# A lane-pipelined attention and MoE kernel: hand-overs between lanes are deferred, whole-array work is gathered into fewer pauses, and the order table is replaced

## The chip, the cores and the metric

The kernel runs on one core of a Trainium2 chip. TensorE (PE) multiplies, VectorE (DVE) and ScalarE (ACT) empty PSUM, GpSimd (POOL) scales the results and issues most of the transfers, and SyncE (SP) issues the others. The time is the device time of one execution in microseconds (us); lower is better. Three executions of the kernel before took 563.68, 565.47 and 568.73 us, so their median is 565.47 us.

## The reference

The input `x` is 4 batches of 12480 tokens with 128 features. There are 32 inducing points, and a feed-forward layer of width 2048 with a PReLU between its two products:

```python
def mab(q, kv):
    s = scale * (q @ kv.transpose(0, 2, 1))
    s = s - s.max(-1, keepdims=True)
    a = np.exp(s)
    a /= a.sum(-1, keepdims=True) + 1e-09
    return a @ kv
h = mab(I, x)                 # 32 rows of 128 for each batch
out = mab(x, h)               # 12480 rows of 128 for each batch
# feed-forward on all 49920 tokens
h = out @ w_in                # 128 -> 2048
g = np.maximum(h, 0.0) + alpha * np.minimum(h, 0.0)
result = g @ w_out            # 2048 -> 128
```

## The kernel before, in words

**The algebra.** For every batch the kernel first makes `h` (32 x 128), then multiplies it with `w_in` (`h_weights`, L458) to `hW`, 16 chunks of 32 x 128. Tokens are worked on in groups of 512, `g`, 24 whole ones and one of 192 in a batch. For a group the exponentials of the 32 scores of each token stand in a tile `rep`, copied four times over the 128 partitions, so that each 32-row strip of the PE array has its own copy. One matmul of 32 rows gives one chunk of the hidden layer, 128 x 512, in a PSUM bank. This is a *fill* (L595). ACT (L613) or DVE (L616) takes the ReLU of it into a `gt` buffer in SBUF. PReLU is split as ReLU times `W1 = (1 - alpha) w_out` plus a linear part, `hA`, that needs no hidden layer (`linear`, L634). The division by the sum of the exponentials comes last: DVE transposes the finished group (L663), POOL multiplies by the reciprocals `rdT` (L666), and four DMAs write it (L680).

**The lanes.** The 32-row strips of the array are four lanes, 0 to 3, that work beside one another. The second product of a group needs 128 rows of every `gt`; each lane holds a quarter. So a group is accumulated in its own PSUM bank in four passes: 16 *pieces* (L620) in lane 0, then 16 in lane 1, and so on. Four groups are under way, each in another lane. Fills are put into whichever lane has room. Since two lanes must not write one bank at once, a group that ends its pass in lane `f` is *handed over*: the kernel places a PE drain that raises the semaphore `fence` (L1061), and the first piece in lane `f + 1` waits for that value (L1054). A drain is declared as fusable. In the built program 261 of 276 hand-overs ride on the last matmul of the pass and 15 stay as an instruction of their own, in front of a PE instruction that waits for something.

**The pauses.** The work for the next batch and for later groups (transposes of `x`, scores, pooling, denominators, `h`) needs the whole array, not lanes. It is put into `tasks` by group number (L844, with the schedule in L860 to L905). When a group starts in lane 0 and its number has such work, all lanes stop, the work runs, and the lanes go on (`pause`, L951, L1012). The 192-token group at the end of a batch (`wholes`, L827 to L832) is also computed on the whole array in such pauses, half of its eight double chunks in one pause and half in the next.

**What sets the order.** A planner inside the kernel (`tokens`, L817) writes out the order of every PE instruction. It keeps rough clocks of PE, ACT and DVE, lists what could be issued next, and takes the earliest. Three knobs for each group (`KNOBS`, L34) say how eager it is to fill, how little must be left of the pass in lane 3 before a fourth group enters, and what a fill costs in a lane that has a pass; the letters of `PLAN` (L35) choose the knobs group by group. Up to `KEPT` = 66 `gt` buffers can be filled ahead. After a hand-over the flag `closed` (L1063) asks for a piece that waits for nothing as the next instruction (a *calm* one); if there is none it takes another. *Warm* matmuls (L1036), 63 of them, write into unused banks while lanes 2 and 3 are still empty.

**Queues.** Each engine runs its instructions in order. SP issues, among others, the copies of exponentials to DRAM and back (`rep`, L516), the reciprocals (`rdT`, L559) and the DMA transposes of `x` (L191); POOL issues the loads of `x` (L177) and nearly all writes of results. The last four groups (L677 to L679) are written by SP, or by SP and ACT in turn.

**The end.** After the last lane pass the last two whole groups and the last 192-token group are computed on the whole array (`tail`, L833).

Of the kernel before, what the change touches and what calls it, by code (L numbers as in the profile page):

```python
# [17 lines left out]
P = 128  # L18
# [6 lines left out]
TAIL = 2  # L25
AHEAD = 8
LAND = 8000
KEPT = 66
RDS = 4
SLOT = 217  # L30
XTS = 8
DONE = 420
SWITCH = 110
KNOBS = [(h, r, c) for h in (300, 450, 600, 800, 1100) for r in (16, 10, 6, 3) for c in (0, 60)]  # L34
PLAN = (  # L35
    "yqbyysrquizoaHqiuiiiobNbizFqbhjiFawqweqiyqiiDbqy"
    "iqqimNqihauihaFicikaebaoaaxiaFbgahiiiaDakiki"
)


# [1 line left out]
def kernel(  # L42
# [9 lines left out]
    nc = tc.nc  # L52
    f32 = mybir.dt.float32
# [80 lines left out]
    def mm(o, lhsT, rhs, start=True, stop=True, **kw):  # L134
        return pin(nc.tensor.matmul(o, lhsT, rhs, start=start, stop=stop, **kw))  # L135
# [302 lines left out]
        st.xn.pop(u)  # L438

    def h_make(st):  # L440
        st.et = work.tile([P, 1], f32, name="et", tag="et")
        pin(nc.vector.tensor_scalar_mul(
            out=st.et[:], in0=st.hacct[:, C : C + 1], scalar1=1.0 / scale
        ))
        ps = bank()
        mm(ps[:, :P], st.hacct[:, :C], fold[:])
        st.hT4 = work.tile([C, P], bf16, name="hT4", tag="hT4")
        pin(nc.vector.tensor_copy(out=st.hT4[:], in_=ps[:, :P]))
        drained(ps, "D", 250, 300)
        st.hT = st.hT4[:, 0:M]  # L450
        ps = bank()
        mm(ps[:, 0:1], fold[:], st.et[:])
        st.rs = work.tile([P, 1], f32, name="rs", tag="rs")
        st.sc = st.rs
        pin(nc.vector.reciprocal(out=st.rs[:], in_=ps[:, 0:1]))
        drained(ps, "D", 150, 100)

    def h_weights(st):  # L458
        st.hW = hw_pool.tile([P, KC, P], bf16, name="hW", tag="hW")
# [108 lines left out]
    begun = set()  # L568
    seen = {}
    held = []  # L570

    def units(g):
        return KC // shape_of(g)[2]
# [78 lines left out]
    def finish(b, g):  # L652
        st = states[b]
        pp, nb, _ = shape_of(g)
        t = pp * nb
        acc = acc_of(b, g)
        s, q = divmod(g, NQ)
        rq = st.rden[s][:, :, :, q : q + 1]
        rbc = bass.AP(
            tensor=rq.tensor, offset=rq.offset, ap=[rq.ap[0], rq.ap[1], rq.ap[2], [0, 32]]  # L660
        )
        ot = ot_pool.tile([P, GRP], f32, name="ot", tag="ot")
        pin(nc.vector.transpose(out=ot[:, :t], in_=acc[:, :t]))  # L663
        drained(accs[b, g], "D", 74 + t * 1.04)
        ob = ob_pool.tile([P, GRP], f32, name="ob", tag="ob")
        pin(nc.gpsimd.tensor_tensor(  # L666
            out=ob[:, :t].rearrange("p (k m c) -> p k m c", k=nb, c=32),
            in0=ot[:, :t].rearrange("p (k m c) -> p k m c", k=nb, c=32),
            in1=rbc, op=MULT,
        ))  # L670
        t0 = b * N + s * SUP
        if s < NS:
            dst = out[t0 : t0 + SUP, :].rearrange(
                "(i b q) (a k) -> q a i b k", b=t // 32, q=NQ, k=32)[q]
        else:
            dst = out[t0 : t0 + REM, :].rearrange("(i b) (a k) -> a i b k", b=t // 32, k=32)
        ending = b == B - 1 and g >= NG - 4  # L677
        for a in range(4):
            eng = (nc.sync, nc.scalar)[a % 2] if ending and g >= NG - 3 else nc.sync if ending else nc.gpsimd  # L679
            pin(eng.dma_start(  # L680
                out=dst[a],
                in_=ob[32 * a : 32 * a + 32, :t].rearrange("p (b k) -> p b k", k=32),
            ))
        st.rep.pop(g)

    order = [0, 1, NS] + list(range(2, NS))
# [130 lines left out]
    def tokens(st):  # L817
# [10 lines left out]
        for b in range(B - 1):  # L828
            c = first[b + 1, 0] - 1
            first[b, NG - 1] = c  # L830
            for u in range(units(NG - 1)):
                wholes[c + u * 2 // units(NG - 1)].append((b, NG - 1, u))  # L832
        tail = [y for y in direct[2:] if y[0] == B - 1]  # L833
        tail.sort()
        need = [((first[y], 1, u), (*y, u)) for y in laned for u in range(KC)]
# [22 lines left out]
        for b in range(B):  # L858
            base = T0 + (first[b, 0] if b else -2)
            for s in range(1, NS + 1):  # L860
                t = base + 4 * s - AHEAD if b or s > 2 else 4 * s - 2
                nt = t + 4 if s < NS else t + 2
                at(t, lambda b=b, s=s: b_scores(states[b], s))
                at(t + 1, lambda b=b, s=s: b_rep(states[b], s))
                at(nt, lambda b=b, s=s: b_den(states[b], s))
                at(nt + 1, lambda b=b, s=s: b_turn(states[b], s))
            if b + 1 < B:
                n = b + 1
                E = base + 4 * NS
                if b:  # L870
                    lag = (-8, -4, -4, 0, 4, 8, 10) if b > 1 else (-4, 0, 0, 4, 6, 8, 10)
                    score = [base + k for k in lag]
                    load = [t - 7 for t in score]
                    cross = [t - 5 for t in score]
                else:
                    score = [T0 + k for k in (2, 4, 4, 6, 9, 11, 13)]
                    load = [0, 0, 5, SESSIONS, T0 + 2, T0 + 4, T0 + 6]
                    cross = [None, None, 6, T0 + 1, T0 + 4, T0 + 6, T0 + 8]
                    at(7, lambda: p_xpose(states[1], 0, 0))
                    at(SESSIONS, lambda: p_xpose(states[1], 0, 1))  # L880
                    at(T0 + 2, lambda: p_xpose(states[1], 1, 0))
                    at(T0 + 3, lambda: p_xpose(states[1], 1, 1))
# [9 lines left out]
                if n == 1:  # L892
                    at(H + 1, lambda n=n: h_make(states[n]))
                    H += 2
                else:
                    at(score[-1] + 1, lambda n=n: h_sum(states[n]))
                    at(H, lambda n=n: h_den(states[n]))
                    at(H + 1, lambda n=n: h_transpose(states[n]))
                    H += 2
                assert H <= E - 6  # L900
                at(H, lambda n=n: h_weights(states[n]))
                at(H, lambda n=n: b_scores(states[n], 0))
# [7 lines left out]
        def run_tasks(t):  # L910
            for fn in tasks.pop(t, []):
                fn()

        prior = []
        for t in range(SESSIONS):
            now = [(0, t // 4, 4 * (t % 4) + f) for f in range(4)]
# [25 lines left out]
        moving = []  # L942
        free_at = [clk.pe] * 4
        gate = {}
        closed = False
        hungry_at, room, cost = 600, KC, 0
        plans = list(PLAN)
        assert len(plans) == len(laned)
        fresh = {f: bank() for f in (2, 3)}
# [1 line left out]
        def pause(t):  # L951
            return t in pauses or (t - T0 < len(wholes) and wholes[t - T0])
# [4 lines left out]
            b, g, _ = need[0]  # L957
            return b in states and g in states[b].rep and hasattr(states[b], "hW")

        while queue or moving or any(tile):  # L960
            best = []
            taken = {q for _, q, _ in moving}
            for f in range(4):
                if tile[f]:
                    y, todo = tile[f]
# [5 lines left out]
                else:  # L971
                    for y, q, t in moving:
                        if q == f:
                            best.append((max(free_at[f], t), 1, f, "enter"))
                    lanes = sum(map(bool, tile)) + len(moving)
                    if f == 0 and queue and lanes < LANES and (
                        lanes < LANES - 1 or room == KC or tile[3] and len(tile[3][1]) <= room
                    ):
# [14 lines left out]
            for f in sorted(fresh):  # L993
                if soon and f not in taken:
                    best.append((free_at[f], 9, f, "warm"))
            assert best, (need[:2], len(seen), tile, moving, queue[:2])
            if closed:
                calm = [x for x in best if x[3] == "piece" and x[2] and x[2] not in gate]
                calm += [x for x in best if x[3] == "warm"]
                best = calm or [x for x in best if x[3] == "piece"] or best  # L1000
            t, _, f, what, *_ = min(best, key=lambda x: (max(x[0], clk.pe) + sum(x[4:]), x[1]))
            if what == "start" and plans:
                m = first[queue[0]]
                if len(laned) - len(plans) == m:
                    hungry_at, room, cost = KNOBS[string.ascii_letters.index(plans.pop(0))]
                    continue
            closed = False
            clk.pe = max(clk.pe, t)
            rows = slice(32 * f, 32 * f + 32)
            if what == "start":  # L1010
                m = first[queue[0]]
# [14 lines left out]
            if what == "enter":  # L1026
# [6 lines left out]
                    clk.free[i] = clk.pe + SLOT  # L1033
                    idle.append(i)
                continue
            if what == "warm":  # L1036
                mm(
                    fresh[f][:], W1[rows, 0, :],
                    W1[rows, 0:NB, :].rearrange("p k c -> p (k c)"), skip_group_check=True,
                )  # L1040
                free_at[f] = clk.pe + SLOT
                continue
            if what == "fill":
                fill(need.pop(0), f)
            else:
# [4 lines left out]
                else:  # L1050
# [7 lines left out]
                    if not todo:  # L1058
                        tile[f] = None
                        if f < 3:  # L1060
                            pin(nc.tensor.drain(fusable=True)).then_inc(fence, 1)  # L1061
                            fenced += 1
                            closed = True  # L1063
                            fences[y, f + 1] = fenced
                            moving.append((y, f + 1, clk.pe + DONE))
                        flush()
            free_at[f] = clk.pe + SLOT
        clk.pe = max(clk.pe, max(free_at) + SWITCH)
        for t in sorted(tasks):
            run_tasks(t)  # L1070
        for y in tail:
# [43 lines left out]
```

## Time and profile before

| | |
|---|---|
| executions | 563.68, 565.47, 568.73 us |
| profiled execution, its own time | 570.99 us |
| its span, first to last instruction | 569.2 us |
| PE busy | 546.6 us (96%), 8860 matmuls |
| ACT busy | 505.3 us (89%) |
| DVE busy | 500.4 us (88%) |
| POOL busy | 408.7 us (72%) |
| mean granted clock of TensorE | 0.988 |
| separate PE drains at L1061 | 15 |

An engine's busy time is the time in which at least one of its instructions was in work. Matmuls overlap, four lanes at a time, so that a busy PE can still have empty lanes: at full pace a 32-row matmul of 512 columns starts every 53 to 54 ns (four in 216 ns), while the profile gives each a duration of 376 ns. ACT takes 617 ns for a full chunk (901 instructions) and DVE 679 ns (635). The granted clock is 1.00 except in short stretches at 0.50.

### The profile page before, as it was taken

Reading aid. Unit: us, or ns where it says so; the run is one execution under the profiler, and the core shown is the slowest. Engines: PE = TensorE matmul, PEld = TensorE weight load, DVE = VectorE, ACT = ScalarE, POOL = GpSimd, SP = SyncE. Lnnn points to the kernel's source line nnn. Section 1 sums busy time; section 2 is a strip of 40 time slices with the busy share of each in tenths; the row PEclk is TensorE's granted clock in tenths of the full one; section 3 lists DMA queues with packets and bytes.
Section 4 is the critical chain, followed back from the end, with each engine's and each line's share of the span. In section 5 each row is a group of like instructions: output and inputs, shape, how many; then the busy total and the mean of one; then the engine's idle time right before and its main releaser. Section 6 shows DMA issues by size and latency. Waiting matters only on the chain.

```text
span 569.2 us, 21360 instructions
## 1 busy us (share of the span) xinstructions
PE 546.6 (96%) x8860; PEld 295.4 (52%) x8864; DVE 500.4 (88%) x861; ACT 505.3 (89%) x1005; POOL 408.7 (72%) x600
## 2 busy tenths in 40 slices
PE   4999997999999999999999999999999999999995
PEld 4645553455455454454555565455555454474642
DVE  3689995899998999999999999999989999999971
ACT  2479995998999999999999999999999999999970
POOL 6646574676688997785987976865778777668681
PEclk9999997999999999999999999999999999999988
DMA  9976999555599997866796894333344244243233
GB/s 198 225 145 125 144 168 157 101 119 82 108 190 159 165 170 142 149 129 107 138 176 123 161 181 115 77 89 68 86 95 113 59 105 102 54 97 66 53 62 62
DMA packets 111201, 69.25 MB, mean 122 GB/s; under 512 B 79824, under 2 KB 101696, under 8 KB 111104
## 3 DMA queue, kind: packets, MB, share of 16 engines
q0 software_dynamic: 23280, 38.53, 36.4%
q1 hardware_dynamic: 85152, 28.52, 26.8%
q8 instruction: 69, 1.13, 0.9%
q10 hardware_dynamic: 2672, 0.84, 0.6%
q14 instruction: 28, 0.23, 0.1%
HBM read 41.00 MB, written 28.95 MB: 123 GB/s over the span
## 4 chain that ended last, share of the span: by engine, by line
POOL 35%; PE 32%; issue 20%; PEld 5%; DVE 4%; DMA 2%; POOLq 0%; SPq 0%; PEldq 0%; ACT 0%; DVEq 0%
PE bank L135 30%; POOL out_dram L680 23%; POOL ob L666 11%; PEld L135 5%; DVE gt L616 2%; PE bank L223 2%; POOL xn L177 1%; DMA ind_f<-in_inducing_dram 1%; DMA rep<-e2d 1%; DVE ot L663 1%; DVE hW L310 1%; DMA out_dram<-ob 0%; DVE xT L229 0%; POOLq L666 0%; PEldq L1061 0%
## 5 line engine op out<-in xcount | busy, mean ns | idle before, releaser
L135 PE MATMUL bank<-gt,W 32*128 32x512 bf16 (+2 forms) x6013 | 490.7, 376 | 4.3 <-issue 3.6
L613 ACT ACTIVATE gt<-bank 128x512 bf16<-128x512 f32 (+1 forms) x920 | 470.2, 615 | 23.9 <-PE bank L135 19.6
L616 DVE TENSOR_SCALAR gt<-bank 128x512 bf16<-128x512 f32 (+1 forms) x648 | 406.6, 677 | 26.8 <-PE bank L135 22.7
L135 PE MATMUL bank<-rep,hW 32*128 32x512 bf16 (+1 forms) x1600 | 415.5, 370 | 2.4 <-DVE hW L310 0.3
L135 PEld LDWEIGHTS <-W 32*128 32x128 bf16 (+1 forms) x6079 | 228.9, 92 | 188.5 <-issue 114.6
L680 POOL DMA_DIRECT2D out_dram<-ob x384 | 246.2, 672 | 43.0 <-POOL ob L666 28.9
L666 POOL TENSOR_TENSOR ob<-ot,rdT 128x512 f32<-128x512 f32 (+1 forms) x100 | 109.4, 1094 | 100.4 <-DVE ot L663 88.8
L135 PEld LDWEIGHTS <-hW 32*128 32x128 bf16 x1600 | 134.0, 92 | 36.7 <-issue 18.6
L663 DVE STREAM_TRANSPOSE ot<-bank 128x512 f32<-128x512 f32 (+1 forms) x100 | 69.7, 698 | 19.0 <-PE bank L135 18.0
L177 POOL DMA_DIRECT2D xn<-in_x_dram x70 | 40.2, 648 | 4.6 <-DMA xn<-in_x_dram 2.4
L135 PE MATMUL bank<-rep,hA 32*128 32x512 bf16 x94 | 35.3, 379 | 0.3 <-DVE hW L310 0.3
L229 DVE COPY xT<-bank 128x1024 bf16<-128x1024 bf16 (+1 forms) x16 | 10.7, 672 | 4.7 <-PE bank L223 4.6
L250 ACT ACTIVATE e1t<-bank 128x256 bf16<-128x256 f32 (+1 forms) x13 | 4.8, 371 | 9.9 <-PE bank L135 8.7
L135 PEld LDWEIGHTS <-hA 32*128 32x128 bf16 x94 | 8.5, 91 | 7.1 <-issue 5.3
L223 PE MATMUL bank<-ident,xn 128*128 128x128 bf16 x128 | 11.3, 242 | 0.9 <-DVE xn L781 0.9
L135 PE MATMUL bank<-xT,hT 128*32 128x512 bf16 (+1 forms) x98 | 10.4, 389 | 0.4 <-ACT gt L613 0.4
L135 PE MATMUL bank<-W 32*128 32x512 bf16 x63 | 10.3, 376 | 0.0
L498 ACT ACTIVATE e<-bank,rs 128x512 bf16<-128x512 f32 x12 | 8.5, 708 | 1.8 <-PE bank L135 1.7
L223 PEld LDWEIGHTS <-xn 128*128 128x128 bf16 x128 | 8.7, 109 | 2.1 <-DVE xn L781 1.0
L498 ACT ACTIVATE e<-bank 128x512 bf16<-128x512 f32 x12 | 7.5, 626 | 1.9 <-PE bank L135 1.8
L135 PE MATMUL bank<-IT,xT 128*128 128x32 bf16 x192 | 8.0, 179 | 0.6 <-issue 0.4
L135 PEld LDWEIGHTS <-e 128*128 128x128 bf16 x96 | 4.3, 96 | 7.4 <-issue 7.4
(100 smaller groups left out, 145.4 us busy)
## 6 DMA issues: line engine op xcount, KB each, us to landing
out_dram<-ob POOLq DMA_DIRECT2D x372, 64.0 KB, 2.7
rep<-e2d SPq DMA_DIRECT2D x92, 128.0 KB, 3.6
xn<-in_x_dram POOLq DMA_DIRECT2D x48, 128.0 KB, 5.8
xn<-in_x_dram POOLq DMA_DIRECT2D x22, 256.0 KB, 7.4
e2d<-e SPq DMA_DIRECT2D x24, 128.0 KB, 2.9
rdT<-rt SPq DMA_DIRECT2D x96, 8.0 KB, 2.2
w_out_f<-in_moe_w_out_dram POOLq DMA_DIRECT2D x4, 256.0 KB, 11.1
xs<-in_x_dram SPq DMA_DIRECT2D x1, 512.0 KB, 5.0
```

Source lines behind the costliest of these rows:

```text
L135: return pin(nc.tensor.matmul(o, lhsT, rhs, start=start, stop=stop, **kw))
L177: pin(nc.gpsimd.dma_start(out=xn[:, i * w : (i + 1) * w, :], in_=src[:, i * w : (i + 1) * w, :]))
L223: pin(nc.tensor.transpose(tp[:, k * P : (k + 1) * P], xn[:, q, j * C : (j + 1) * C], ident[:]))
L229: pin(nc.vector.tensor_copy(out=dst, in_=tp[:, :w]))
L250: pin(nc.scalar.activation(out=e1t[:pp, :nb, :].rearrange("p k m -> p (k m)"), in_=ps[:pp, : nb * M], func=EXP, scale=scale,))
L310: pin(nc.vector.tensor_scalar(out=out, in0=in_, scalar1=st.rs[:, 0:1], scalar2=1.0 / scale, op0=MULT, op1=MULT,))
L498: pin(nc.scalar.activation(out=e2[:].rearrange("p (t j i) -> p t j i", j=n, i=32), in_=turned(ps[:pp, :w], n), func=EXP, scale=scale_of(st ...
L613: pin(nc.scalar.activation(out=gt[:, :w], in_=ps[:, :w], func=RELU))
L616: pin(nc.vector.tensor_relu(gt[:, :w], ps[:, :w]))
L663: pin(nc.vector.transpose(out=ot[:, :t], in_=acc[:, :t]))
L666: pin(nc.gpsimd.tensor_tensor(out=ob[:, :t].rearrange("p (k m c) -> p k m c", k=nb, c=32), in0=ot[:, :t].rearrange("p (k m c) -> p k m c", ...
L680: pin(eng.dma_start(out=dst[a], in_=ob[32 * a : 32 * a + 32, :t].rearrange("p (b k) -> p b k", k=32),))
```

## The change

- **Hand-overs.** A finished pass goes into a list `owed`. `hand_over()` places the drain just before the next calm matmul (a piece that waits for nothing, a warm or a spare one), before a pause, or when nothing else can be issued. A fourth knob, `at_once`, lets a group hand over without a calm matmul, and the planner's clock then counts `DRAIN` = 270 ns.
- **Pauses.** Tasks are moved by one or two group numbers so that they share a pause; the eight double chunks of a 192-token group go into one pause instead of two. Loads and transposes of `x` move by up to two groups.
- **Buffers and table.** `KEPT` 66 to 62, `XTS` (buffers for transposed `x`) 8 to 9; new `KNOBS` and a new `PLAN`. The planner is told that groups 2 and 3 of batch 0 land at 9000 ns.
- **The end.** While the last pieces run, *spare* matmuls with no use fill the lanes below. Of the four DMAs that write the last 512-token group (`NG - 2` of the last batch), two are kept back and issued by POOL after those of the last 192-token group (`NG - 1`).
- **h_make** (the first pass over batch 1's sums) multiplies by the scale after the reciprocal instead of before the matmul.

```diff
-KEPT = 66
+KEPT = 62
-XTS = 8
+XTS = 9
+DRAIN = 270
-KNOBS = [(h, r, c) for h in (300, 450, 600, 800, 1100) for r in (16, 10, 6, 3) for c in (0, 60)]
+KNOBS = [
+    (h, r, c, d) for h in (300, 450, 600, 800) for r in (16, 6, 3) for c in (0, 60) for d in (0, 1)
+]
...
     def h_make(st):
-        st.et = work.tile([P, 1], f32, name="et", tag="et")
-        pin(nc.vector.tensor_scalar_mul(
-            out=st.et[:], in0=st.hacct[:, C : C + 1], scalar1=1.0 / scale
-        ))
...
-        mm(ps[:, 0:1], fold[:], st.et[:])
+        mm(ps[:, 0:1], fold[:], st.hacct[:, C : C + 1])
...
+        pin(nc.vector.tensor_scalar_mul(out=st.rs[:], in0=st.rs[:], scalar1=scale))
...
+            src = ob[32 * a : 32 * a + 32, :t].rearrange("p (b k) -> p b k", k=32)
+            if b == B - 1 and g == NG - 2 and a > 1:
+                late.append((dst[a], src))
+            else:
+                pin(eng.dma_start(out=dst[a], in_=src))
+        if b == B - 1 and g == NG - 1:
+            for dst, src in late:
+                pin(nc.gpsimd.dma_start(out=dst, in_=src))
...
-                wholes[c + u * 2 // units(NG - 1)].append((b, NG - 1, u))
+                wholes[c + 1].append((b, NG - 1, u))
...
-                t = base + 4 * s - AHEAD if b or s > 2 else 4 * s - 2
-                nt = t + 4 if s < NS else t + 2
+                t = base + 4 * s - AHEAD - (b == 0 and s > 4) if b or s > 2 else 4 * s - 2
+                nt = t + (5 if b == 0 and s == 2 else 3 if b == 0 and s == 4 else 4 if s < NS or b + 1 < B else 2)
...
-                    lag = (-8, -4, -4, 0, 4, 8, 10) if b > 1 else (-4, 0, 0, 4, 6, 8, 10)
+                    lag = (-8, -4, -4, 0, 4, 8, 8) if b > 1 else (-4, 0, 0, 4, 4, 8, 8)
-                    load = [t - 7 for t in score]
-                    cross = [t - 5 for t in score]
+                    load = [t + k - 7 for t, k in zip(score, (0, 0, 2, 0, 1, 0, 2))]
+                    cross = [t + k - 5 for t, k in zip(score, (0, 0, 1, 0, 1, 0, 2))]
...
-                    cross = [None, None, 6, T0 + 1, T0 + 4, T0 + 6, T0 + 8]
+                    cross = [None, None, 6, T0 + 1, T0 + 4, T0 + 7, T0 + 8]
...
-                    at(H + 1, lambda n=n: h_transpose(states[n]))
-                    H += 2
+                    at(H + 2, lambda n=n: h_transpose(states[n]))
+                    H += 4
...
+        landed.update({(0, g): 9000 for g in (2, 3)})
...
+        def hand_over():
+            nonlocal fenced
+            if owed:
+                pin(nc.tensor.drain(fusable=True)).then_inc(fence, 1)
+                fenced += 1
+            for y, f in owed:
+                fences[y, f + 1] = fenced
+                moving.append((y, f + 1, clk.pe + DONE))
+            owed.clear()
...
+            if not queue and not need:
+                low = min([f for f in range(4) if tile[f]] + sorted(taken), default=4)
+                for f in range(low):
+                    best.append((free_at[f], 9, f, "spare"))
+            calm = [x for x in best if x[3] == "piece" and x[2] and x[2] not in gate]
+            calm += [x for x in best if x[3] in ("warm", "spare")]
+            if owed and not best:
+                hand_over()
+                continue
+            if owed and not calm and at_once:
+                hand_over()
+                clk.pe += DRAIN
+                continue
...
-            if closed:
-                calm = [x for x in best if x[3] == "piece" and x[2] and x[2] not in gate]
-                calm += [x for x in best if x[3] == "warm"]
-                best = calm or [x for x in best if x[3] == "piece"] or best
+            if owed and calm:
+                best = calm
...
+            if best is calm or what == "start" and pause(T0 + first[queue[0]]):
+                hand_over()
...
-                            pin(nc.tensor.drain(fusable=True)).then_inc(fence, 1)
-                            fenced += 1
-                            closed = True
-                            fences[y, f + 1] = fenced
-                            moving.append((y, f + 1, clk.pe + DONE))
+                            owed.append((y, f))
```

More of the change, by code (lines that the diff above doesn't have):

```diff
@@ L27 @@
 LAND = 8000
-KEPT = 66
+KEPT = 62
 RDS = 4
 SLOT = 217
-XTS = 8
+XTS = 9
 DONE = 420
 SWITCH = 110
-KNOBS = [(h, r, c) for h in (300, 450, 600, 800, 1100) for r in (16, 10, 6, 3) for c in (0, 60)]
+DRAIN = 270
+KNOBS = [
+    (h, r, c, d) for h in (300, 450, 600, 800) for r in (16, 6, 3) for c in (0, 60) for d in (0, 1)
+]
 PLAN = (
-    "yqbyysrquizoaHqiuiiiobNbizFqbhjiFawqweqiyqiiDbqy"
-    "iqqimNqihauihaFicikaebaoaaxiaFbgahiiiaDakiki"
+    "aaKKfGcyLqmADMamiiznjafamQcyaqcafqanqaxacmOaav"
+    "AmnCamKeacfymraaJmRnAynqyauaNmmgadjmafycQazyAm"
 )
@@ L455, in h_make @@
         pin(nc.vector.reciprocal(out=st.rs[:], in_=ps[:, 0:1]))
-        drained(ps, "D", 150, 100)
+        pin(nc.vector.tensor_scalar_mul(out=st.rs[:], in0=st.rs[:], scalar1=scale))
+        drained(ps, "D", 250, 100)
     def h_weights(st):
@@ L570 @@
     held = []
+    late = []
     def units(g):
@@ L679, in finish @@
             eng = (nc.sync, nc.scalar)[a % 2] if ending and g >= NG - 3 else nc.sync if ending else nc.gpsimd
[L680 to L683, printed above, removed]
+            src = ob[32 * a : 32 * a + 32, :t].rearrange("p (b k) -> p b k", k=32)
[6 more added lines that the diff above has]
+                pin(nc.gpsimd.dma_start(out=dst, in_=src))
         st.rep.pop(g)
@@ L944, in tokens @@
         gate = {}
-        closed = False
-        hungry_at, room, cost = 600, KC, 0
+        owed = []
+        hungry_at, room, cost, at_once = 600, KC, 0, 0
         plans = list(PLAN)
@@ L958, in fillable @@
             return b in states and g in states[b].rep and hasattr(states[b], "hW")
-        while queue or moving or any(tile):
+        def hand_over():
[7 more added lines that the diff above has]
+            owed.clear()
+        while queue or moving or owed or any(tile):
             best = []
-            taken = {q for _, q, _ in moving}
+            taken = {q for _, q, _ in moving} | {f + 1 for _, f in owed}
             for f in range(4):
@@ L974, in tokens @@
                             best.append((max(free_at[f], t), 1, f, "enter"))
-                    lanes = sum(map(bool, tile)) + len(moving)
+                    lanes = sum(map(bool, tile)) + len(moving) + len(owed)
                     if f == 0 and queue and lanes < LANES and (
@@ L1004, in tokens @@
                 if len(laned) - len(plans) == m:
-                    hungry_at, room, cost = KNOBS[string.ascii_letters.index(plans.pop(0))]
+                    hungry_at, room, cost, at_once = KNOBS[string.ascii_letters.index(plans.pop(0))]
                     continue
-            closed = False
             clk.pe = max(clk.pe, t)
+            if best is calm or what == "start" and pause(T0 + first[queue[0]]):
+                hand_over()
             rows = slice(32 * f, 32 * f + 32)
@@ L1035, in tokens @@
                 continue
-            if what == "warm":
+            if what == "spare" and f not in fresh:
+                fresh[f] = bank()
+            if what in ("warm", "spare"):
                 mm(
@@ L1068, in tokens @@
         clk.pe = max(clk.pe, max(free_at) + SWITCH)
+        for f in sorted(fresh):
+            i = number[id(fresh.pop(f))]
+            clk.free[i] = clk.pe
+            idle.append(i)
         for t in sorted(tasks):
```

## The prediction

> **What bounds the kernel now.** I read the stretches first, then the waits inside the lanes, then single pauses and drains on PE. The busy time by stretches (columns: stretch, its length, busy us and instructions of PE, weight loads, DVE, ACT and POOL, granted clock, DMA share, GB/s):
>
> ```profile
> 220.00:240.00 20.00, 19.85 (x346) 9.32 (x342) 19.25 (x34) 19.55 (x41) 16.28 (x25) 1.00 0.88 153
> 88.30:91.90 3.60, 0.36 (x6) 0.00 (x0) 0.97 (x2) 1.04 (x3) 0.62 (x1) 0.87 0.96 212
> 91.00:97.70 6.70, 5.77 (x55) 2.88 (x57) 2.69 (x4) 2.88 (x6) 1.99 (x4) 0.50 0.93 211
> 548.30:551.70 3.40, 3.38 (x33) 1.49 (x31) 2.81 (x6) 3.07 (x8) 2.76 (x5) 1.00 0.39 82
> 551.70:555.10 3.40, 3.18 (x9) 1.05 (x9) 0.72 (x1) 0.00 (x0) 3.31 (x5) 0.50 0.38 77
> ```
>
> In the middle (first row) ACT and DVE are both nearly full: 0.45 and 0.75 us of idle in 20. PE is not: 346 matmuls of mostly 53 ns are some 17 us of lane time. So a bubble on PE costs only what ACT and DVE idle for it. The other rows are two places where the clock is halved; I come back to them. The waits from 100 to 548 us, the lane stage:
>
> ```profile
> DVE gt L616 <- PE bank L135: 12.3, 38, 1.0
> ACT gt L613 <- PE bank L135: 8.9, 24, 1.6
> DVE ot L663 <- PE bank L135: 8.7, 24, 0.9
> ```
>
> ACT and DVE wait for PE and hardly for anything else. Adding up every gap between their instructions in this stage gives 16.7 us of idle on ACT and 28.0 on DVE. Whose fault? One pause and one separate drain, PE alone:
>
> ```profile
> 323.46 0.53 PE L135 MATMUL bank<-gt,W 32*128 32x512 bf16 x3
> 323.92 0.25 PE L135 MATMUL bank<-pick,e 128*128 128x4 bf16 x4
> ...
> 324.56 0.39 PE L135 MATMUL bank<-xT,IT 128*32 128x512 bf16 x4
> 324.88 0.38 PE L135 MATMUL bank<-rep,hA 32*128 32x512 bf16 x1
> ```
> ```profile
> 481.62 0.87 PE L135 MATMUL bank<-gt,W 32*128 32x512 bf16 x3
> 482.11 0.39 PE L135 MATMUL bank<-rep,hW 32*128 32x512 bf16 x1
> ```
> ```profile
> L1061 PEldq DRAIN  x15: 517/653/1003, 85.2 to 543.8; - x15
> ```
>
> At the pause, the last lane matmul starts at 323.62 (the third of its row) and the first whole-array one at 323.92: 0.31 us instead of 0.053, a loss of 0.25; coming back takes another 0.31 from a row of four matmuls that needs 0.21, a loss of 0.10. One turn there and back costs PE about 0.35 us. Next to the drain there is a hole of 0.48 us (from the last of the three at 481.62 to 482.11): 0.43 us lost. I did this for all. The trace has 38 whole-array stretches after 95 us, 43.3 us in all (1.14 each); the ACT and DVE gaps over 0.1 us around them come to 0.38 us a stretch as a mean of the two engines, and a line through the 38 points gives 0.23 us + 0.13 x length. Around the 14 drains in the stage the same sum is 3.38 us for ACT and 4.29 for DVE, 0.27 us a drain. Pauses are 14.4 of the 22.4 us of mean idle: the largest prize, and the change goes for them.
>
> **The change part by part.** The built order of the changed kernel gives the counts.
>
> *Pauses.* Whole-array stretches among the lanes fall from 40 to 30; the matmuls in them are the same. Each stretch saved is worth 0.23 us, and 10 turns of 0.35 us shorten the total length, x 0.13: 2.3 + 0.5 = **2.8 us** gained. The bounds are all of PE's turns (10 x 0.35 = 3.5 gained) and a loss of 4.1 (first rival).
>
> *Drains.* The change defers hand-overs so that the drain can ride on a matmul, but the built order has 19 separate drains, not 15: 254 of 273 ride, where 261 of 276 did. Eight of the 19 (two before) stand right ahead of the piece that waits for their own fence; those two show the same hole, 0.48 and 0.52 us. Four more at 0.27: **1.1 us** lost, between 0 (ACT and DVE covered) and 4 x 0.43 = 1.7. Only a dozen matmuls stand between a finished pass and its held hand-over, at most 0.2 us for the group each; lanes have that much room, so I count nothing, and 12 x 0.2 = 2.4 if they had not.
>
> *Who empties.* ACT gets four full and one short chunk more (4 x 617 + 543 ns = 3.0 us), DVE three full and one short fewer (2.6 us). Their mean grows by **0.2 us**. If ACT alone set the pace it would be 3.0 less its share of the pauses (11.4 us of idle at 37 pauses in the stage, x 10 = 3.1) plus four drains (1.0): +0.9 in place of -1.5 for the stage.
>
> *Buffers, loads, transposes.* The `x` loads and transposes that move stay at least three groups (some 15 us at about 5 us a group) ahead of their scores, against medians of 5.8 to 7.4 us for a load and 6.8 for a transpose; One transpose now follows its load by one group only, so that SP may hold 2 us on it; the `rep` queued behind is needed three groups later. Nothing, while that cover holds; a late one stops PE in order, 1 us for each us. Four `gt` buffers fewer is a quarter of a group of look-ahead in some four: nothing. The new table reorders fills; of the mean idle 22.4 - 14.4 - 3.8 = 4.2 us belongs to neither pauses nor drains, and that is all that an order can gain or, doubled, lose. I take 0. In SP's queue, one transpose of `x` moves from ahead of `rdT` and `rep` (77.01, 81.46 and 83.52 us) to behind them.
>
> *h_make.* One tiny DVE multiply moves from before a matmul to after a reciprocal: 0, within 0.4 us (PE waited 0.4 for it).
>
> *The end.* In the fourth row above, PE starts 33 matmuls in 3.4 us where the middle has 59: one lane works alone. In the next 3.4 us the clock is 0.50, and the whole-array matmuls of the tail start every 427 ns, eight of them, not every 216. PE is what the tail waits for, so this costs 8 x 0.211 = 1.7 us. The change puts 21 spare matmuls, in three lanes, beside the last eight pieces; three of them wait for banks, emptied before. With 54 starts instead of 33 I expect the clock to stay: **1.7 us** gained, between 0 and 2.2 (with the 0.46 us gap in front). By the Trainium skill, "TensorE: Matmul & The Clock Gate", Part 1, the clock is halved after an idle window of about 3.4 us. Here PE was busy for 3.38 of 3.40 us and the clock fell all the same, so the trace speaks for a count of activity; by the page's rule as it stands the spare matmuls would change nothing.
>
> *Last writes.* After the last POOL multiply (ends 563.58) SP and ACT issue four writes each, 0.6 us apiece; SP holds from 564.37 to 565.65 for an earlier transfer to land and ends at 566.94; the last lands near 568.2. With two writes moved to POOL, SP and ACT are done near 565.0, POOL (0.67 each) near 565.0 too, and its last lands 2.7 us after its issue, near 567.1: **1.0 us** gained, between 0 and 1.3.
>
> *Sum:* -2.8 + 1.1 + 0.2 - 1.7 - 1.0 = **-4.2 us**.
>
> **From which time?** The profiled execution took 570.99 us (span 569.2 plus 1.8 around it), 5.5 over the median. Rows two and three tell why: at 88.3 PE, ACT and DVE all stop for 3.6 us without a wait, then the clock is 0.50 until 97.7. That is 3.4 us of stop and about 2.9 of half pace, 6.2 in all; without it the profile would be near 564.8. In the trace's list of packets PE's 16 KB blocks of instructions start at 77.85 and 89.12, mostly 6 to 10 us apart elsewhere, while the DMA share is near 1. So I hold that the runs near the median lack this stop, take it as neither gained nor lost, and predict 565.47 - 4.2 = **561.3 us**. Against its own time the profile would go to 566.8 with the stop and 560.6 without.
>
> **Rivals.**
>
> 1. *Longer pauses outlast the cover (slower).* Two mean stretches, merged, last 2 x 1.14 - 0.35 = 1.93 us. If ACT and DVE are fed for a fixed 0.76 us (1.14 - 0.38) and idle for all beyond, the merged one costs 1.17, the two cost 0.76: ten of them +4.1 instead of -2.8, in all +2.7, **568.2 us**. It decides as soon as stretches are longer than 0.76 us, and the merged ones have up to 48 matmuls. Against it: stretches of 2.0 to 2.5 us (at 140, 173, 262, 305 and 389 us) idle 0.2 to 0.6, so the slope is 0.13 and not 1.
> 2. *The turns count in full:* PE is what everything waits for. -3.5 with no price for drains and the upper ends of clock and writes (-2.2, -1.3), +0.2: -6.8, **558.7**. For it: the waits above all name PE. Against: the line's low slope.
> 3. *The stop for instructions in most runs of the changed kernel:* 561.3 + 6.2 = **567.5**; or in most runs before and none after, 555.1. DMA is as full at 60 to 100 us in both. The page "Runtime: NRT & Kernel Launch" of the Trainium skill, Instruction fetch mechanics, calls the fetch mostly hidden; here it is not.
> 4. *The clock falls after an idle window only,* and the tail stays at half clock: -2.5, **563.0**.
>
> **How the numbers follow.** The forecast has 0.42, rival 1 0.15, rival 2 0.14, rival 3 0.10 up and 0.05 down, rival 4 0.14. The range takes in rival 2 and the upward rivals with up to 1.5 us for held hand-overs: **557 to 569**. About 1% (5.7 us) is what three runs 0.9% apart can tell from no change. Faster by over 1% is below 559.8: rival 2, rival 3 down, and a tenth from the spread of the forecast, **0.30**. Slower by over 1% is above 571.1: rivals 1 and 3 together, or a late transfer that stops PE, **0.13**. Within 1%: **0.57**.
>
> **What would show it.** Right: 30 whole-array stretches; idle of ACT and DVE in the lanes lower by 2 to 3 us as a mean; 19 drains; no 0.50 at the tail and matmuls there 216 ns apart; the last write landing 4.1 us after the last DVE transpose instead of 5.3. Wrong: idle at the merged pauses in step with their length, ACT full and DVE idle, or a stop of all engines in another place.

## The result: 559.73 us, 0.986 of the kernel before

The changed kernel took 559.73 us (median of four executions, 558.86 to 560.04) against 565.58 (four, 563.68 to 568.73): 5.85 us less, a ratio of 0.9863 with a 95% interval of 0.9818 to 0.9908. The forecast was 561.3, in a range of 557 to 569. With its own runs of the kernel before, a second comparison on another chip gave 559.28 us and 0.985 (0.980 to 0.990).

The number of the kernel before needs a second look. The experiments below brought 67 more executions of it on four chips. In half of them (34) the mean granted clock is 0.985 to 0.991 and the time 568 to 575 us (median 571.0), as in the profiled execution shown above; in the other 33 it is 0.992 to 0.999 and the time 562 to 570. The changed kernel shows no such split: its ten executions lie between 558.9 and 560.6 us, with clocks of 0.996 to 0.998. The four executions behind 565.58 lie mostly in the better half; the medians of the four chips are 565.5 to 570.7, so that against them the same change is worth 6 to 11 us.

The profile of the changed kernel (its own time 558.86, span 557.1) in the stretches that answer to those of before; columns as there. The last two rows are the 3.4 us before and after the start of the whole-array tail.

```profile
88.30:91.90 3.60, 3.60 (x67) 2.12 (x63) 3.47 (x6) 3.60 (x8) 0.12 (x1) 1.00 1.32 166
91.00:97.70 6.70, 6.70 (x138) 3.87 (x132) 5.87 (x12) 6.58 (x14) 4.16 (x6) 1.00 0.80 132
220.00:240.00 20.00, 19.89 (x363) 10.26 (x359) 18.67 (x34) 19.24 (x39) 14.70 (x23) 1.00 0.75 158
538.40:541.80 3.40, 3.40 (x48) 1.45 (x47) 2.04 (x5) 2.76 (x7) 3.10 (x6) 1.00 0.38 77
541.80:545.20 3.40, 3.35 (x16) 1.52 (x16) 0.72 (x1) 0.00 (x0) 3.02 (x4) 1.00 0.38 77
```

The stop at 88 us is gone (67 matmuls in those 3.6 us instead of 6), with the half clock behind it. The tail runs at full clock, 16 matmuls in 3.4 us instead of 9. The middle looks as before. The waits in the lane stage, 100 to 540 us:

```profile
DVE gt L617 <- PE bank L138: 12.0, 35, 0.6
...
DVE ot L664 <- PE bank L138: 6.9, 16, 1.3
ACT gt L614 <- PE bank L138: 5.4, 18, 0.7
```

ACT waits less for PE (5.4 us instead of 8.9), DVE a little less (18.9 us in its two rows instead of 21.0). The separate drains, and a pause that now holds what two held (the 192-token group of a batch with the tasks behind it), PE alone:

```profile
L969 PEldq DRAIN  x19: 417/548/868, 107.1 to 486.1; - x19
```
```profile
293.79 0.54 PE L138 MATMUL bank<-gt,W 32*128 32x512 bf16 x3
294.26 0.26 PE L138 MATMUL bank<-rep,hAq 128*128 128x192 bf16 x1
294.36 1.48 PE L138 MATMUL bank<-gt,W 128*128 128x192 bf16 x16
295.68 0.24 PE L138 MATMUL bank<-pick,e 128*128 128x4 bf16 x4
...
296.39 0.41 PE L138 MATMUL bank<-xT,IT 128*32 128x512 bf16 x4
296.73 0.39 PE L138 MATMUL bank<-rep,hA 32*128 32x512 bf16 x1
```

One long stretch, 2.77 us from the last lane matmul to the next, where the kernel before had two of 1.03 and 2.02. That is some 0.3 us less on PE: one turn.

Between the two profiled executions the span falls by 12.1 us. By landmarks: the twentieth group starts in lane 0 at 138.3 instead of 147.0 us, the tail starts at 541.7 instead of 552.1, the tail takes PE 8.9 us instead of 10.4, and from the last DVE transpose to the end it is 6.0 instead of 6.2. So 10.4 us come from the stage of lanes (the stop among them), 1.5 from the tail, 0.2 from the end.

### The profile page after: what moved, and what is told of

Read it like the earlier page. It is cut to its first block, busy times and chain, and to the rows that moved or that the text cites. A ratio compares the mean times of both kernels' runs of the same rounds, so it can differ in the third digit from the quotient of the medians.

```text
span 557.1 us, 21434 instructions
## 1 busy us (share of the span) xinstructions
PE 538.6 (97%) x8890; PEld 293.1 (53%) x8894; DVE 497.3 (89%) x858; ACT 503.8 (90%) x1008; POOL 411.4 (74%) x602
## 4 chain that ended last, share of the span: by engine, by line
PE 31%; issue 27%; PEld 25%; POOL 8%; DMA 4%; ACT 3%; DVE 1%; PEldq 1%; POOLq 0%; DVEq 0%
PE bank L138 31%; PEld L138 25%; POOL out_dram L685 5%; DMA xn<-in_x_dram 3%; POOL ob L667 3%; ACT gt L614 2%; PEldq L969 1%; PE bank L226 1%; DMA out_dram<-ob 1%; DVE gt L617 1%; DVE hW L313 0%; POOL xn L180 0%; DVE ot L664 0%; DMA rt<-rd 0%; PEld bank L138 0%
## 5 line engine op out<-in xcount | busy, mean ns | idle before, releaser
L138 PE MATMUL bank<-gt,W 32*128 32x512 bf16 (+1 forms) x6013 | 482.9, 374 | 1.6 <-DVE gt L617 0.3
L667 POOL TENSOR_TENSOR ob<-ot,rdT 128x512 f32<-128x512 f32 (+1 forms) x100 | 111.0, 1110 | 93.5 <-DVE ot L664 83.7
L138 PEld LDWEIGHTS <-hW 32*128 32x128 bf16 x1600 | 135.6, 91 | 31.3 <-issue 15.1
L138 PE MATMUL bank<-W 32*128 32x512 bf16 x93 | 13.8, 376 | 0.0
L138 PE MATMUL bank<-xT,hT 128*32 128x512 bf16 (+1 forms) x98 | 10.4, 389 | 0.6 <-ACT gt L614 0.4
L138 PEld LDWEIGHTS <-hT 128*32 128x32 bf16 (+1 forms) x122 | 5.0, 93 | 5.8 <-issue 4.0
```

Of the source, the lines that this page charges most:

```text
L667: pin(nc.gpsimd.tensor_tensor(out=ob[:, :t].rearrange("p (k m c) -> p k m c", k=nb, c=32), in0=ot[:, :t].rearrange("p (k m c) -> p k m c", ...
```

## The experiments

### The changed kernel again, and its end: spare matmuls and last writes

The first is the yardstick. The second takes the spare matmuls out, the third puts the four writes of the last 512-token group back on SP and ACT:

```diff
-            if not queue and not need:
+            if False:
                 low = min([f for f in range(4) if tile[f]] + sorted(taken), default=4)
```
```diff
-            if b == B - 1 and g == NG - 2 and a > 1:
+            if False:
```

> The changed kernel once more, as the yardstick for the others on one chip. Expected: 559.7 us (558.9 to 560.0 so far), 0.986 of the kernel before, no stretch at half clock in the lanes or in the tail.

> The changed kernel without the 20 spare matmuls beside the last pieces. If activity in a window of 3.4 us holds the clock (forecast), the tail falls to half clock again and the kernel is 1.5 to 1.7 us slower than the changed one (561.3). If only an idle window halves the clock (rival 4), the tail stays at full clock and nothing changes (559.7).

> The changed kernel with the four writes of the last 512-token group on SP and ACT again. By the forecast's step: 1.0 us slower (560.7). By the profile of the changed kernel, where the end stands 6.0 us behind the last DVE transpose instead of 6.2: 0.2 us slower (559.9). If the drain of POOL at the end (4.3 us there) is the price of writes issued by POOL: faster by up to 0.5.

Measured: 559.28 us (six executions) for the changed kernel, 559.20 without spare matmuls, 559.20 with the old writes. The medians do not differ. For the writes that is the answer: moving two of them to POOL is worth nothing. In the profile of the changed kernel the last transfers do land earlier (4.5 us after the last DVE transpose, where it was 5.3), but POOL's own closing drain, which now begins behind two transfers of its own, lasts until 5.2 us after that transpose and the end waits for it; with the old writes the end stood 5.6 us behind the transpose, with the new ones 6.0.

For the spare matmuls the median hides something. The profiled execution without them kept its clock:

```profile
538.90:542.30 3.40, 3.40 (x31) 1.25 (x25) 2.31 (x5) 3.02 (x8) 3.10 (x5) 1.00 0.38 77
542.30:545.70 3.40, 3.35 (x16) 1.58 (x17) 0.72 (x1) 0.00 (x0) 3.29 (x5) 1.00 0.38 77
```

31 matmuls in the 3.4 us before the tail, as few as the 33 of the kernel before, and yet 1.00 in the tail. But of the six executions two have a mean clock of 0.994 and 560.7 and 561.0 us, four have 0.996 to 0.998 and 558.6 to 559.5. Two of six against none of six would not settle it; all runs of this study do. With spare matmuls 0 of 49 executions have a clock of 0.9945 or less; in the three kernels without them whose profile shows no stop at 88 us, 9 of 24 do. Those are 1.5 to 2.1 us slower, and a half-clock stretch of 3.4 us in 560 is 0.003 of the mean clock, which is the step seen. So the spare matmuls do prevent the fall, but without them it comes in some two executions of five and not in each.

The traces show on what it depends. In all 14 the granted clock changes only at a whole number of steps of 3.413 us (in the kernel before the changes are 78.51, 6.83, 453.97, 3.41 and 10.24 us apart), and this grid lies in another place against the program in each execution. Give each matmul the time for which it would fill the array at full pace (0.053 us for 32 rows and 512 columns, 0.213 us for 128 rows, others in proportion), and add up what starts in each step of the grid. All 19 falls from full to half clock in the 14 traces (14 of them at the very end, where PE has nothing left to do) come after a step with at most 1.17 us of such work; none of the 2249 steps that full clock outlasted holds less than 1.28. Ahead of the tail the step with least work held 1.17 us in the kernel before, with 32 starts and PE busy for all of it, and 1.28 in the execution without spare matmuls shown here: there the grid cut the thin stretch at 541.5 us, and its second part shares a step with the tail. With spare matmuls the least is 1.5. A kernel below without spare matmuls (the one called "with the new schedule alone") fell in its profile; the rows are one step of the grid each:

```profile
560.11:563.52 3.41, 3.41 (x31) 1.32 (x27) 2.63 (x6) 2.85 (x7) 2.44 (x4) 1.00 0.28 58
563.52:566.94 3.42, 3.20 (x9) 1.07 (x9) 0.72 (x1) 0.00 (x0) 2.94 (x4) 0.50 0.38 77
```

In the first row PE is busy throughout; 28 of its 31 matmuls start in it, 1.09 us of work. The Trainium skill says in "TensorE: Matmul & The Clock Gate", Part 1, that the window of 3.4 us runs freely; the grid in the traces agrees.

### The stop at 88 us: the place of one transpose in SP's queue

The kernel before with one edit:

```diff
-                    cross = [None, None, 6, T0 + 1, T0 + 4, T0 + 6, T0 + 8]
+                    cross = [None, None, 6, T0 + 1, T0 + 4, T0 + 7, T0 + 8]
```

> The kernel before with one edit: the sixth transpose of x for batch 1 is issued one group later, behind the rdT and rep transfers on SP instead of ahead of them. About half of the executions of the kernel before show a mean clock of 0.986 to 0.991 and 570 to 575 us, the others 0.994 to 0.999 and 563 to 567. If the order on SP makes the stop near 88 us (theory A), all executions are of the second kind: clock at least 0.993, median 565. If the amount of DMA makes it, whatever its order (theory B), half of them still stop: median 567 to 568 and clocks of 0.988 among them.

Measured: 562.95 us (twelve executions, 562.1 to 565.8), 0.9965 (0.993 to 0.9997) of the kernel before, which had 565.53 (562.3 to 571.6, eight of 23 at clocks of 0.988 to 0.991). None of the twelve is below 0.992. Theory A holds against theory B: with the same amount of DMA the place of this transpose makes the stop. The edit moves it behind the small transfers and to a later time at once, so that order and time are not told apart. SP's queue in the kernel before and in this one (start, us, line, transfer):

```profile
77.01 4.36 SPq L191 DMA_TRANSPOSE xT<-xn  x1
81.46 1.95 SPq L559 DMA_DIRECT2D rdT<-rt  x4
83.52 8.53 SPq L516 DMA_DIRECT2D rep<-e2d  x4
93.04 2.44 SPq L191 DMA_TRANSPOSE xT<-xn  x1
```
```profile
80.24 1.89 SPq L559 DMA_DIRECT2D rdT<-rt  x4
82.24 2.36 SPq L516 DMA_DIRECT2D rep<-e2d  x4
85.49 6.01 SPq L191 DMA_TRANSPOSE xT<-xn  x2
```

With the transpose ahead, issuing the four copies of `rep` takes 8.5 us and all engines stand still from 88 us; behind them, the copies are issued in 2.4 us. Two more kernels of this study (both below) keep the transpose ahead, and both stop in their profiles: the one with the new schedule of pauses and the old table for 3.5 us at 88.0, and the kernel before with one setting of the knobs for 2.7 us at 90.0. This one (SP's queue, then the busy time by stretch, columns as above):

```profile
78.29 4.92 SPq L191 DMA_TRANSPOSE xT<-xn  x1
85.73 7.08 SPq L516 DMA_DIRECT2D rep<-e2d  x4
```
```profile
87.50:92.00 4.50, 2.90 (x45) 1.44 (x40) 3.45 (x6) 3.31 (x7) 3.38 (x5) 1.00 1.18 205
```

Here the grid of 3.413 us cut the stop, 1.65 us of work were left in the poorer step, and the clock stayed. So an execution can have the stop without the half clock, and the half of the executions with a low clock is a lower bound for the stop. The 11 traces with the transpose behind have none.

What PE stands still for shows in the list of packets. In the three traces that stop, a 16 KB block of PE's instructions starts at 89.12, 88.87 and 90.28 us, 11 to 12 us after the one before it; in the 11 others it starts between 82.0 and 85.8, 5 to 8 us after. PE goes on 1.47, 1.44 and 1.52 us after the late block has landed. That it waits for this block is therefore likely; no run delays the block alone.

The profile of the kernel with one edit is also what the first comparison lacked, the kernel before without the stop and with full clock at the tail. From the first `hA` matmul in a lane to the first matmul of the tail it takes 505.1 us; four profiles with the lanes of the changed kernel (two of itself, one without spare matmuls, one with the old writes) take 502.0 to 502.9. So the undisturbed gain of the lane stage, without stop and half clock, is 2.2 to 3.1 us, **2.7** as a mean, and by the medians the changed kernel is 3.5 us faster than this one (559.4, the mean of its two medians). The other 2.6 us, from 565.58 to 562.95, are the stop and part of the tail's clock.

### What a turn, a longer pause and a separate drain cost

Three edits of the changed kernel. None changes what is computed; extra matmuls write into banks that the next fill overwrites (`fresh_bank()` gives the idle bank that is free first).

```diff
                 else:
                     run_tasks(T0 + m)
+                    if m > 12 and not m % 2:
+                        i = fresh_bank()
+                        mm(banks[i][:, :16], W1[:, 0, :], W1[:, 1, :16], skip_group_check=True)
```
```diff
                     run_tasks(T0 + m)
+                    i = min(idle, key=lambda i: clk.free[i])
+                    for _ in range(3):
+                        mm(banks[i][:], W1[:, 0, :], ..., skip_group_check=True)
                     clk.pe += SWITCH
```
```diff
-                pin(nc.tensor.drain(fusable=True)).then_inc(fence, 1)
+                pin(nc.tensor.drain(fusable=fenced % 4 != 0)).then_inc(fence, 1)
```

> The changed kernel with 16 more turns: at 16 group starts without a pause, one whole-array matmul of 16 columns stands between lane matmuls (its result is not used). Forecast (0.23 us + 0.13 x length): 16 x 0.28 = 4.5 us slower. All of PE's time counts (rival 2): 16 x 0.4 = 6.4. The line through the pauses of the changed kernel's profile (0.02 + 0.30 x length): 16 x 0.14 = 2.2. A fixed cover of 0.76 us (rival 1): 0.

> The changed kernel with every pause made longer by three whole-array matmuls of 512 columns (0.65 us; results not used); 32 pauses, 20.8 us of PE in all. Forecast (slope 0.13): 2.7 us slower. The line of the changed kernel's profile (slope 0.30): 6.2. A fixed cover of 0.76 us, already used up by a mean pause of 1.4 us (rival 1), or PE as the bound (rival 2): near 20.

> The changed kernel with every fourth hand-over declared as not fusable, in the same order: 82 separate drains instead of 19. Forecast (0.27 us a drain): 63 x 0.27 = 17 us slower. PE's whole hole of 0.43: 27. By the idle around the 19 drains in the changed kernel's profile (0.10 a drain): 6.

Measured against 559.4 us (the mean of the two medians of the changed kernel; that of 559.28 is from another chip):

| edit | time | more | each |
|---|---|---|---|
| 16 more turns | 563.44 | 4.0 | 0.25 us a turn |
| 32 pauses, 0.65 us longer | 580.93 | 21.5 | 1.03 us for 1 us |
| 63 more separate drains | 580.80 | 21.4 | 0.34 us a drain |

The price of a turn was foreseen (0.28) and so, less well, that of a drain (0.27). The slope of 0.13 us for each us of pause was not: a pause that grows by matmuls whose results nobody empties costs nearly all that it grows. (In the trace the 32 pauses grew by 22.7 us together, a little more than planned, so that the price is 0.95 us for 1 us.) The waits of the kernel with long pauses, 100 to 560 us, show the extra time on both engines:

```profile
DVE gt L617 <- PE bank L138: 26.1, 35, 1.3
...
ACT gt L614 <- PE bank L138: 22.6, 39, 1.1
DVE ot L664 <- PE bank L138: 11.2, 17, 1.3
```

Against 12.0, 5.4 and 6.9 these are 35.6 us more on two engines, 18 each, for 21.5 us of span. Pause by pause, the gaps of ACT and DVE over 0.1 us, from the last lane matmul ahead of a pause to 1 us behind it, grew by 0.89 us (mean of the two engines) for each us that the pause grew. PE's time counts nearly in full, as rival 2 said, for drains to 0.34 of 0.43 and for turns to 0.25 of 0.42 (one lane matmul to the next around the added one).

### Schedule, hand-over and table apart

First the old table with the new schedule of pauses, then the new table with the old hand-over. In the first the marks of a cut stand for the lines of the change that move pauses, loads and transposes; the line with `T0 + 6` stays as it was:

```diff
 (kernel before)
-KEPT = 66
+KEPT = 62
...
-XTS = 8
+XTS = 9
...
-                wholes[c + u * 2 // units(NG - 1)].append((b, NG - 1, u))
+                wholes[c + 1].append((b, NG - 1, u))
...
```
```diff
 (changed kernel)
                             owed.append((y, f))
+                            hand_over()
+                            closed = True
...
-            if owed and calm:
-                best = calm
+            if closed:
+                best = calm or [x for x in best if x[3] == "piece"] or best
```

> The kernel before with only the new schedule of pauses and loads (and the buffer counts 62 and 9): 30 whole-array stretches instead of 40, 8 separate drains instead of 15, its old table and old hand-over, no spare matmuls. If a stretch saved is worth 0.28 us and a drain 0.27 (forecast): 565.5 - 2.8 - 1.9 = 560.8. If merged pauses outlast the cover (rival 1): +4.1 - 1.9, 567.7. If the gain of the lane stage came from the new table: 565.5.

> The changed kernel with the hand-over of the kernel before (drain placed at once, a calm matmul asked for next, no at_once); schedule, table and end as changed. 3 separate drains instead of 19, none in front of the piece that waits for it. By the measured price of a drain (0.34 us): 16 x 0.34 = 5.4 us faster, 554. If the table was fitted to the new hand-over and pays for its drains with a better order elsewhere: as slow as or slower than the changed kernel, 559.5 to 565.

Measured: the kernel before with the new pauses 571.01 us, 1.009 (1.005 to 1.013) of the kernel before, and 568.6 at best; the changed kernel with the old hand-over 573.73 us, 14 us more than the changed kernel, although it has 3 separate drains instead of 19. Both are slower than anything that was expected. Neither number need be what its edit costs: the table picks the knobs group by group for one particular stream of instructions, and a stream that differs early differs behind. So I gave all groups one setting and compared without a table; the second of the three kernels has the schedule above and the line with `T0 + 7`:

```diff
-                    hungry_at, room, cost, at_once = KNOBS[string.ascii_letters.index(plans.pop(0))]
+                    hungry_at, room, cost, at_once = (plans.pop(0), (450, KC, 0, 0))[1]
```

> The kernel before with one setting of the knobs (450, 16, 0) for all groups instead of its table; 40 stretches, 9 separate drains. If the table is worth little: 565 less 6 drains x 0.34 = 563. If the table carries the order: 5 to 15 us slower, 570 to 580.

> The changed kernel with the same single setting (450, 16, 0, no at_once); 30 stretches, 1 separate drain. Against the kernel before with that setting this is what schedule, hand-over and end are worth without a table. Forecast: 10 turns x 0.25, 8 drains x 0.34 and 0.6 at the tail, 5.8 us faster than that one. If the gain of the changed kernel came from the new table alone: no faster than that one.

> The kernel before with the single knob setting (450, 16, 0) for all groups and the new schedule of pauses, loads and transposes (buffer counts 62 and 9), old hand-over, old end: 30 stretches and 9 separate drains, against 40 and 9 of the kernel before with that setting (585.5 us). Ten turns fewer at the measured 0.25 us: 583.0. By the forecast's 2.8: 582.7; what is left to the changed kernel with that setting (582.35, 1 drain) would then be the hand-over's, 8 x 0.34 = 2.7 at the most. If merged pauses outlast the cover (rival 1): 589.6. If merging changes nothing: 585.5.

| one setting for all groups | stretches | drains | time (all executions) |
|---|---|---|---|
| kernel before | 40 | 9 | 585.49 (583.2 to 586.9) |
| with the new schedule alone | 30 | 9 | 582.31 (580.8 to 582.5) |
| the changed kernel | 30 | 1 | 582.35 (581.7 to 582.7) |

The first is slower than was expected, the second as expected; the third was to be 5.8 us below the first and is 3.1. The first two differ by 3.2 us, but not by pauses alone. The profile of the first has the stop of 2.7 us shown above, and the second moves the transpose that makes it. The second has the tail at half clock in its profile, where PE takes 10.4 us for the tail instead of 8.9, and by their clocks (0.994 and 0.995) in four of its six executions. Without either, the first would take some 583.1 us (the 585.68 of its profiled execution less 2.6; its best took 583.2), the second 580.9 (its two executions at 0.997 and 0.998), and the third 582.35. So the schedule, with the transposes that it moves, gives about 2.3 us, and hand-over and end take about 1.4 of it back with this setting, although eight separate drains fall away. These differences rest on one trace or two executions each and may be off by 1 us.

Against this setting a fitted table is worth 20 to 23 us in both kernels. With tables the changed kernel keeps 2.7 to 3.5 us undisturbed, without them about 0.8. How much of the rest is due to the new table, and how much to a hand-over that needs it, no run tells: the new schedule with the old table loses 5 to 6 us, and the new table without its hand-over 14.

## Why the prediction was right, and where it was not

**The sum.** Forecast -4.2 us and 561.3; measured -5.85 and 559.73. About 2.6 of it are the stop and part of the tail's clock, which the kernel with one edit sheds too, and 3.2 the lanes and the tail. That the total came near is in part luck: the drains (1.1 lost) did not show, the last writes (1.0 gained) came out as nothing, and the two cancel; and the stop, taken as nothing, put in what the tail's clock did not. By the number alone rival 2 lay nearer (558.7).

**Pauses, 2.8 us: right in size.** 2.3 by the schedule alone with the stop taken out, and ten turns at the measured 0.25 us are 2.5. But the slope in it was wrong, and with it the reason given against rivals 1 and 2. The line through the pauses (0.13 us of idle for each us of length) mixes length and content: a longer pause also hands ACT and DVE more work of its own, exponentials and copies. In the trace of the kernel before, the time of that work goes with the length of the pause (correlation 0.82), and while the gaps as counted above give 0.14 by length alone, a fit with both gives 0.54 us of idle for each us of length and 0.44 less for each us of own work. Added length that feeds nobody idles the engines 0.89 us for each us, and costs 0.95. Merging drops turns and adds no length, so the wrong slope touched only 0.5 of the 2.8.

Busy time is also not the load of these engines. ACT in two kernels, with no idle in either stretch (start, us, chunks):

```profile
224.87 3.65 ACT L614 ACTIVATE gt<-bank 128x512 bf16<-128x512 f32 x7
```
```profile
224.72 7.37 ACT L614 ACTIVATE gt<-bank 128x512 bf16<-128x512 f32 x13
```

The first is the changed kernel: 7 chunks in 3.65 us, or 0.51 us from start to start if the last takes 0.62. The second is the changed kernel with one setting: 13 in 7.37, 0.56 from start to start. Both are "busy" all the time. An instruction of 0.62 us can follow the last after 0.48 us (the lower quartile of the starts in both), so when PE feeds ACT late the instructions draw apart before any idle appears. From 100 to 540 us, where ACT is 97% busy in the changed kernel, the starts of chunks that follow one another lie 27 us further apart than that in sum, 6% of the stretch; with one setting it is 52 us of the 460 from 100 to 560.

**Drains, 1.1 us lost: the price was near, the sum did not show it.** 0.34 us instead of 0.27. Yet the changed kernel has four more than the one before and is not slower for it, with 16 fewer it was 14 us slower, and with one setting eight fewer did not make it faster. The number of separate drains was not what decided; the order of all else, which changes with the hand-over, weighed more, and what in it no run tells.

**Who empties, 0.2 us lost: miscounted.** In the traces ACT gets two full chunks and one short one more, not four and one, and DVE as many fewer: 1.8 us on one and 1.9 on the other, nothing as a mean.

**Buffers and table, 0 within 4.2 us: right in the net, wrong in the bound.** The table swings 20 us, not 4.2. That the net came out small may be because each kernel has a fitted one.

**The tail's clock, 1.7 us: the size is right, the frequency is not.** It costs 1.5 to 2.1 us, in 9 of 24 executions without spare matmuls. For the median of the changed kernel it is 0. Rival 4 named the time (its term at zero), not for its reason: the clock fell after a step in which PE was busy throughout. The reading of the forecast, that activity counts, holds.

**Last writes, 1.0 us: wrong.** 0.0, since the end then waits for POOL's closing drain. The step looked at when transfers land and not at what else POOL does before the program ends.

**The stop, neither gained nor lost: wrong.** It was in at least half of the executions, and the move of one transpose, which the prediction listed and priced at nothing, takes it away. Rival 3 had this downward case with 0.05. It is also why the result lies below the forecast rather than above it, with two terms that came out empty.

**Rival 1** (a fixed cover of 0.76 us, then one for one) had the right slope for long pauses and the wrong sign for the change: a turn of 0.4 us costs 0.25, so there is little cover, and merging two pauses saves a turn and adds no length.

## What to carry to other kernels

A line through stretches of different content prices the content as well as the length. Make the suspected bound 0.65 us worse in some thirty places and see how much comes back. Busy shares of an engine whose instructions overlap say little about its limit: read its pace from start to start. Before a profiled execution is used for a sum, compare its time and its mean clock with those of other executions, and look in every profile for the same stop; here it weighed as much as the lanes, and it stood in one of the kernels that were built to measure something else. An order that was searched for one stream must be searched again for every change to it, and what a structural edit is worth is best measured with the search left out on both sides.

## What the runs showed of the hardware that was not expected

- One DMA transpose ahead of eight small transfers in SP's queue, at a time when the DMA share was near 1, went with a slow issue of four copies (6.0 to 8.5 us instead of 1.7 to 2.6) and a stop of PE, ACT and DVE of 2.7 to 3.6 us, in all three traces that have it there. One group later it did neither (11 traces). PE went on 1.4 to 1.5 us after a late 16 KB block of its instructions had landed.
- The clock of TensorE can fall to half with PE busy 3.41 of 3.41 us. In the 14 traces full clock ended after every step of a grid of 3.413 us with at most 1.17 us of array work, 19 times, and after none with 1.28 or more. Matmuls of no use beside a lone lane kept it up: 0 of 49 executions with them fell, 9 of 24 without.
- A PE drain that stays an instruction of its own costs 0.34 us more than one that rides on a matmul (63 made separate, 21.4 us), next to a hole of 0.48 us on PE.
